# FNet mixing and a squared-ReLU layer on one core: the folds of a batch spread over three blocks, and P−Q+N taken on VectorE in other steps

## The chip, the cores and the metric

The kernel runs on one core of a Trainium2 chip. The metric is the device time of one execution, in microseconds (us). The profile is of one execution of the kernel before the change, taken by the hardware profiler. Its engines are PE (TensorE matmuls), PEld (TensorE weight loads), DVE (VectorE), ACT (ScalarE), POOL (GpSimd) and SP (SyncE, here the queue of output stores).

## The reference

```python
# x: 8 x 3008 x 256, w_in: 256 x 2048, w_out: 2048 x 256, all float32
X = np.fft.fft(x, axis=1)          # over the 3008 positions
X = np.fft.fft(X, axis=2)          # over the 256 features
t = X.real.reshape(8 * 3008, 256)
h = np.maximum(t @ w_in, 0.0)
out = h * h @ w_out                # 24064 x 256
```

## The kernel before, in words

**What is computed how.** The transform over the features is multiplied into `w_in` once, at the start (`gh`, 256 x 2048, as a cosine part, a sine part, and a third part `gh[:, 2]` that is minus twice the sine part but for one row). The transform over positions is done as matmuls with tables of cosines and sines, after the 3008 positions have been folded by symmetry (position n with position S−n, then the halves once more). Rows k and S−k of the result differ only in the sign of the sine product: with P the cosine product and Q the sine product, one row needs P+Q and the other P−Q, with a term N (the Nyquist feature) that keeps its sign. So only about half of the columns are computed, 12040 in all, and each column gives two output rows.

**Blocks and steps.** The columns are cut into 25 blocks ("windows" in the code, `wins`, index `w`): 240, 512, 512, 240, 512, 448 columns, then 18 blocks of 512, and a last one of 360. Each block has 8 steps `s` (`NST`), and a step makes 256 of the 2048 hidden features for all its columns: `phs[s]`, a PSUM tile `ph` of two banks, of which there are two. A step is written out in this order, and every engine works through its share of the program in order:

- A **plain step**: `pq` (two pairs of matmuls, lines 793 and 794, P+Q into `ph`); `settle` (VectorE squares what earlier steps left in the list `kept`, `power`, line 833, and what `held` kept back is done by `let_go`); `relu(s, 0)` on ScalarE (line 829); `others(s)`, see below; `turn` (two matmuls, line 816, which add the third part and so make P−Q+N); `relu(s, 1)` on ScalarE. That is six matmuls of the block's width. In step 7 the first half is squared at once, ahead of `others(7)`, and only the second half goes to `kept`.
- A **step in `diff[w]`** takes P−Q+N on VectorE: `cosines` (two matmuls, line 802, P alone); `twice` on VectorE (line 806: `t2` = n2 − 2P, from PSUM); `settle`; `others(s)`; `sines` (two matmuls, line 811, which wait for `twice`, since they add Q to the tile that it reads); `relu(s, 0)` on ScalarE; `relu(s, 1)` on VectorE (line 827: `t2` + (P+Q), cut at zero). That is four matmuls, and the second ScalarE operation is gone. The tile `n2` is made by GpSimd, two operations a step (line 739, in `nyq_rows`), from a row that a matmul with `sel` spreads over the partitions (line 730) and ScalarE copies (line 731), in step 6 of the block before (`hi`) for the first step of `diff`, and in step 7 for the others. There are three buffers for `n2`.
- **`others(s)`**: the fold jobs `at[s]`; then 16 matmuls (line 678, `ffn2_steps`) of the second layer for 128 rows of the block before, whose sum ScalarE copies out every second step (line 693) and SP stores; then `post[s]`; then a share of the position transform of the next block (`z_steps`, line 565, copies on ScalarE, and `minus` on VectorE, line 594), spread over the steps from `lo` up to, not including, `hi`.

**The folds.** The columns of a batch i (order in the code, 0 to 7) come in two units, (i, 0) and (i, 1). For i from 2 on, unit (i, 0) begins in block b0 + 2 where b0 is 5, 8, 10, 13, 16 and 19. The jobs of `fold_steps(i)` are: `d_even` (lines 417 to 419), `n_cos` (427), `d_odd` (422; it ends by issuing the load of the next batch's x on GpSimd's queue, lines 127 to 150), `n_sin` (430), `odds` (433), `nyq` (438 to 440: two tiny matmuls and a copy), `even` (445, and a write to scratch memory in DRAM on GpSimd's queue, 447), `back` (four reads of it on the same queue, 455 and 457, which wait for the write), and the four `late` jobs (471 twice, 482 twice, and with the last the small copies of lines 488 to 490), which need what `back` read. Before the change all but the late ones lie in block b0: `d_even`, `n_cos`, `d_odd`, `n_sin` in steps 0 to 3, `odds` in 5, `even` and then `nyq` in 6, `back` in 7. The late jobs lie in steps 2, 4, 6 and 7 of the second block ahead of the unit (i, 1): blocks 6, 9, 12, 15, 18, 21 (`late_at`).

**Which steps are in `diff`:** (4, 6) in block 4, (5,) in the fold blocks b0, and (2, 4, 6) in all others from block 6 on: 50 steps.

Of the kernel before, what the change touches and what calls it, by code (L numbers as in the profile page):

```python
# [29 lines left out]
def kernel(  # L30
# [15 lines left out]
    B, S, D = x.shape  # L46
    _, F = moe_w_in.shape
# [7 lines left out]
    NFC = F // P  # L55
# [24 lines left out]
    NW = len(wins)  # L80

    def win_of(col):
        return max(w for w in range(NW) if wins[w][0] <= col) if col < TOT else NW
# [5 lines left out]
    col_of = {}  # L89
# [218 lines left out]
    at = const.tile([P, 2, P + 1], F32, name="at")  # L308
# [228 lines left out]
    held = {"on": False, "jobs": []}  # L537

    def let_go():
        jobs, held["jobs"] = held["jobs"], []  # L540
        for j in jobs:
            j()
# [167 lines left out]
    folds = {0: f0s}  # L710

    def fold_jobs(i):
        f = folds[i] = fold_steps(i)
        return [f["d_even"], f["n_cos"], f["d_odd"], f["n_sin"], f["odds"], f["nyq"], f["even"], f["back"]]

    fold_at, late_at = {}, {}
    for i in range(2, B):
        fold_at[win_of(col_of[i, 0]) - 2] = i
        late_at[win_of(col_of[i, 1]) - 2] = i
    NST = NFC // 2  # L720
    diff = {w: (4, 6) if w == 4 else (5,) if w in fold_at else (2, 4, 6) for w in range(4, NW)}
    n2s = {}
    BIG = 3.0e38
    zns = {}

    def spread_nyq(wt):
# [15 lines left out]
    for w in range(NW):  # L742
        g0, wn = wins[w]
        h2 = h2p.tile([P, NFC, 2 * WN], F16, name="h2", tag="h2")
        zcw, zsw = zwin(w)

        lo, hi = 0, NST - 2
        at = [[] for _ in range(NST)]
        post = [[] for _ in range(NST)]
        if w == 0:  # L750
            at[0] = [lambda: gh_step(2, True), lambda: gh_turn(2), f0s["v_even"]]
            at[2] = [lambda: gh_step(3, False), lambda: gh_turn(3)]
            rm = z0(0, 2) + z0(1, 2)
            at[4] = rm[0::2]
            at[5] = rm[1::2]
        elif w == 1:
            fj = fold_jobs(1)
            at = [[], fj[0:1], fj[1:2], fj[2:3], fj[3:5], [], [], []]
            post[5] = fj[5:6]
            lo, hi = 6, NST  # L760
        elif w == 2:
            te = table_steps(1)
            at = [[folds[1]["even"]], [lambda: te["freq"](), lambda: te["args"](0)], [lambda: f0s["v_part"](0)], [lambda: f0s["v_part"](1), f0s["even"], f0s["back"]],
                  [lambda: te["turns"](0)], [lambda: te["mods"](0)], [lambda: te["absm"](0), lambda: te["sins"](0)], [lambda: te["coss"](0)]]
        elif w == 3:
            at[0] = [lambda: te["weigh"]()]
            for st in range(4):
                at[1 + st // 2] = at[1 + st // 2] + f0s["late"][st : st + 1]
            at[3] = [folds[1]["back"]]
            lo, hi = 4, NST  # L770
        elif w in fold_at:
            fj = fold_jobs(fold_at[w])
            at = [[f] for f in fj[0:4]] + [[], fj[4:5], fj[6:7], fj[7:8]]
            post[6] = fj[5:6]
        elif w == win_of(col_of[1, 1]) - 1:
            for st in range(4):
                at[1 + st] = folds[1]["late"][st : st + 1]
            lo, hi = 5, NST
        if w in late_at:
            for st in range(4):  # L780
                at[(2, 4, 6, 7)[st]] += folds[late_at[w]]["late"][st : st + 1]
        zj, zl = [], []
        for u in need[w + 1]:
            zu = z_steps(u)
            zj += [(zu, 1, 0), (zu, 0, 0), (zu, 1, 1), (zu, 0, 1)]
        f2 = ffn2_steps(*old) if old else []
        phs = {}

        def pq(s):
            ph = phs[s] = ps_h.tile([P, 2, 512], F32, name="ph", tag="psh")  # L790
            for a in range(2):
                f0 = (2 * s + a) * P
                nc.tensor.matmul(ph[:, a, 0:wn], gh[:, 0, f0 : f0 + P], zcw[:, 0:wn], start=True, stop=False)  # L793
                nc.tensor.matmul(ph[:, a, 0:wn], gh[:, 1, f0 : f0 + P], zsw[:, 0:wn], start=False, stop=True)  # L794

        t2s = {}

        def cosines(s):
            ph = phs[s] = ps_h.tile([P, 2, 512], F32, name="ph", tag="psh")
            for a in range(2):  # L800
                f0 = (2 * s + a) * P
                nc.tensor.matmul(ph[:, a, 0:wn], gh[:, 0, f0 : f0 + P], zcw[:, 0:wn], start=True, stop=True)  # L802

        def twice(s):
            t2 = t2s[s] = tmp.tile([P, 3 * NE], F32, name="t2", tag="tt")[:, 0 : 2 * WN].rearrange("p (a n) -> p a n", a=2)
            nc.vector.scalar_tensor_tensor(out=t2[:, :, 0:wn], in0=phs[s][:, :, 0:wn], scalar=-2.0, in1=n2s[w, s][:, :, 0:wn], op0=ALU.mult, op1=ALU.add)  # L806

        def sines(s):
            for a in range(2):
                f0 = (2 * s + a) * P  # L810
                nc.tensor.matmul(phs[s][:, a, 0:wn], gh[:, 1, f0 : f0 + P], zsw[:, 0:wn], start=False, stop=True, skip_group_check=True)  # L811

        def turn(s):
            for a in range(2):
                f0 = (2 * s + a) * P
                nc.tensor.matmul(phs[s][:, a, 0:wn], gh[:, 2, f0 : f0 + P], zsw[:, 0:wn], start=False, stop=True, skip_group_check=True)  # L816

        def relu(s, sg):
            h = h2[:, 2 * s : 2 * s + 2, sg * wn : (sg + 1) * wn]
            if sg:  # L820
                h = rev_dim(h, 2)
            if w == 1 and not sg:

                for a in range(2):
                    nc.scalar.activation(h[:, a], phs[s][:, a, 0:wn], AF.Relu, bias=0.0, scale=-1.0)  # L825
            elif sg and s in t2s:
                nc.vector._custom_dve(TENSOR_ADD_SAT, out=h, in0=t2s[s][:, :, 0:wn], in1=phs[s][:, :, 0:wn], s0=BIG, s1=0.0)  # L827
            else:
                nc.scalar.activation(h, phs[s][:, :, 0:wn], AF.Relu, bias=0.0, scale=-1.0)  # L829

        def power(s, a, b):
            h = h2[:, 2 * s : 2 * s + 2, a * wn : b * wn]
            nc.vector.tensor_tensor(h, h, h, op=ALU.mult)  # L833

        def others(s):
            for j in at[s]:
                j()
            for j in spread(f2, s, NST):
                j()
            for j in post[s]:  # L840
                j()
            if s == lo:
                zl[:] = [j for zu, part, h in zj for j in zu(part, h)]
            if s >= lo:
                for j in spread(zl, s - lo, hi - lo) if s < hi else []:
                    j()

        def nyq(s):
            if w + 1 in diff and hi < NST - 1:
                if s == hi:  # L850
                    spread_nyq(w + 1)
                    nyq_rows(w + 1, diff[w + 1][0:1])
                elif s == hi + 1:
                    nyq_rows(w + 1, diff[w + 1][1:])
            if s == 0 and w in diff and w not in zns:
                spread_nyq(w)
                nyq_rows(w, diff[w])

        kept = []

        def settle():
            for k in kept:
                power(*k)
            kept.clear()
            let_go()

        ng = 2 if w == 0 else 1
        for s0 in range(0, NST, ng):
            ss = range(s0, s0 + ng)
            held["on"] = s0 + ng in diff.get(w, ())  # L870
            if s0 in diff.get(w, ()):
                cosines(s0)
                twice(s0)
                settle()
                others(s0)
                sines(s0)
                relu(s0, 0)
                relu(s0, 1)
                kept.append((s0, 0, 2))
                nyq(s0)  # L880
                continue
            for s in ss:
                pq(s)
            settle()
            for s in ss:
                relu(s, 0)
                if s == NST - 1:
                    power(s, 0, 1)
            for s in ss:
                others(s)  # L890
            nyq(s0)
            for s in ss:
                turn(s)
            for s in ss:
                relu(s, 1)
                kept.append((s, int(s == NST - 1), 2))
        held["on"] = False
        settle()
        if w == 0:
            gh_nyq()  # L900
        old = (w, h2)
# [32 lines left out]
```

## Time and profile before

| | |
|---|---|
| median of three runs | 625.15 us (625.14 to 625.29) |
| the profiled execution: time, span | 625.18 us, 623.4 us |
| PE busy | 599.6 us (96%), 4487 matmuls |
| DVE busy | 464.3 us (74%) |
| ACT busy | 423.3 us (68%) |
| POOL busy | 257.1 us (41%) |
| clock granted to TensorE | 0.998 |

Times in the profile count from the start of the span. The profiled execution takes 1.78 us more than its span, and 0.03 us more than the median. Matmuls are pipelined: the duration of one (379 ns for 512 columns) is longer than the distance to the next, so work on PE is costed by the distance between starts. "Idle before" is what the engine waited ahead of a group, and the arrow names what ended that wait.

### The profile page before, as it was taken

The page shows a single profiled execution, that of the slowest core. Times are in us where ns is not written, and L with a number is a line of the kernel's source. Part 1 is how long each engine was busy: PE and PEld are TensorE (multiplying, and loading weights), DVE is VectorE, ACT ScalarE, POOL GpSimd, SP SyncE. Part 2 cuts the span into 40 slices and gives each one's busy share as a digit, 9 for nine tenths or more (in the row PEclk, how much of TensorE's full clock was granted, in tenths as well). Part 3 has the DMA queues.
Part 4 walks back from the last instruction along what each step waited for, and adds up shares of the span by engine and source line. Part 5 has one row for each costly group of instructions (what it writes and reads, how often), then busy time and mean ns, then how long its engine had stood idle before and what let it go on. Part 6 is the DMA issues. An engine that isn't in the chain of part 4 may idle for free.

```text
span 623.4 us, 11238 instructions
## 1 busy us (share of the span) xinstructions
PE 599.6 (96%) x4487; PEld 431.3 (69%) x4487; DVE 464.3 (74%) x567; ACT 423.3 (68%) x589; POOL 257.1 (41%) x202
## 2 busy tenths in 40 slices
PE   4789998899999999999999999999999999999997
PEld 2456686577677777777777777776777777777786
DVE  7686753886978869768788679876797787876761
ACT  6677766767767666776677675776667767666652
POOL 8302322356452292255422942347610446426310
PEclk9999999999999999999999999999999999999999
DMA  8746331136111731541116411173111221211112
GB/s 151 106 99 142 103 95 35 33 68 163 49 46 34 150 99 50 109 124 49 52 46 121 119 47 43 44 143 102 50 29 62 68 79 34 51 44 37 53 54 68
DMA packets 36539, 47.51 MB, mean 76 GB/s; under 512 B 4231, under 2 KB 30343, under 8 KB 36487
## 3 DMA queue, kind: packets, MB, share of 16 engines
q0 software_dynamic: 9344, 22.14, 17.8%
q1 hardware_dynamic: 26915, 24.44, 13.1%
q8 instruction: 35, 0.57, 0.4%
q10 hardware_dynamic: 228, 0.21, 0.1%
q14 instruction: 17, 0.14, 0.1%
HBM read 33.63 MB, written 27.84 MB: 99 GB/s over the span
## 4 chain that ended last, share of the span: by engine, by line
PE 86%; ACT 5%; DVE 3%; POOL 3%; DMA 1%; issue 1%; POOLq 0%; DVEq 0%
PE po L678 49%; PE ph L816 9%; PE ph L793 9%; PE ph L794 9%; PE pz L565 3%; PE ph L811 3%; PE ph L802 3%; ACT h L829 3%; DMA scr<-ev 1%; ACT h L825 1%; DVE t L806 1%; PE pn L730 1%; POOL n L739 1%; DVE h L833 1%; PE pg L511 0%
## 5 line engine op out<-in xcount | busy, mean ns | idle before, releaser
L829 ACT ACTIVATE h<-ph 128x1024 f16<-128x1024 f32 (+3 forms) x342 | 317.3, 968 | 83.4 <-PE ph L816 39.7
L678 PE MATMUL po<-wout,h 128*128 128x256 f16 (+1 forms) x3024 | 361.6, 273 | 0.0
L678 PEld LDWEIGHTS <-h 128*128 128x128 f16 (+1 forms) x3024 | 296.5, 98 | 71.6
L833 DVE TENSOR_TENSOR h<-h 128x2048 f16<-128x2048 f16 (+7 forms) x225 | 235.4, 1057 | 80.8 <-ACT h L829 78.8
L739 POOL TENSOR_SCALAR n<-zn,g2n 128x512 f32<-128x512 f16 (+2 forms) x100 | 179.5, 1810 | 169.4 <-ACT zn L731 169.0
L793 PE MATMUL ph<-zc,gh 128*128 128x512 f16 (+3 forms) x300 | 108.0, 363 | 5.4 <-DVE zc L594 2.2
L794 PE MATMUL ph<-zs,gh 128*128 128x512 f16 (+3 forms) x300 | 108.0, 363 | 0.0
L693 ACT ACTIVATE osb<-po 128x512 f32<-128x512 f32 (+2 forms) x94 | 54.9, 587 | 64.3 <-PE po L678 50.8
L816 PE MATMUL ph<-zs,gh 128*128 128x512 f16 (+3 forms) x300 | 84.2, 363 | 3.4 <-ACT h L825 1.9
L806 DVE SCALAR_TENSOR_TENSOR t<-ph,n 128x1024 f32<-128x1024 f32 (+2 forms) x50 | 60.1, 1203 | 33.3 <-PE ph L802 30.2
L827 DVE CUSTOM_DVE_ANT_0 h<-t,ph 128x1024 f16<-128x1024 f32 x46 | 56.1, 1220 | 16.6 <-ACT h L829 15.3
L794 PEld LDWEIGHTS <-gh 128*128 128x128 f16 x300 | 29.3, 98 | 37.4 <-issue 6.7
L793 PEld LDWEIGHTS <-gh 128*128 128x128 f16 x300 | 29.2, 98 | 31.0 <-DVE h L827 0.2
L816 PEld LDWEIGHTS <-gh 128*128 128x128 f16 x300 | 27.5, 97 | 12.2 <-issue 6.0
L447 POOL DMA_DIRECT2D scr<-ev x8 | 4.8, 596 | 65.9 <-DVE od L440 49.2
L811 PE MATMUL ph<-zs,gh 128*128 128x512 f16 (+2 forms) x100 | 29.3, 374 | 1.6 <-DVE t L806 1.6
L802 PE MATMUL ph<-zc,gh 128*128 128x512 f16 (+2 forms) x100 | 29.3, 375 | 0.0
L127 POOL DMA_DIRECT2D xo<-in_x_dram x8 | 6.3, 782 | 52.9 <-DVE fo L422 42.4
L570 ACT ACTIVATE es<-pz 128x376 f32<-128x376 f32 (+1 forms) x32 | 15.3, 483 | 13.8 <-PE pz L565 13.7
L132 POOL DMA_INDIRECT xo<-in_x_dram,idx_r x15 | 21.1, 1407 | 4.5 <-issue 4.3
L457 POOL DMA_INDIRECT rb<-scr,idx_r x16 | 19.8, 1237 | 4.9 <-issue 4.9
L802 PEld LDWEIGHTS <-gh 128*128 128x128 f16 x100 | 9.8, 98 | 11.4
(134 smaller groups left out, 338.5 us busy)
## 6 DMA issues: line engine op xcount, KB each, us to landing
out_dram<-osb SPq DMA_DIRECT2D x77, 128.0 KB
xo<-in_x_dram POOLq DMA_DIRECT2D x7, 768.0 KB, 6.7
scr<-ev POOLq DMA_DIRECT2D x8, 390.0 KB, 3.7
rb<-scr POOLq DMA_DIRECT2D x16, 130.0 KB
out_dram<-osb SPq DMA_DIRECT2D x12, 94.0 KB
w<-in_moe_w_in_dram POOLq DMA_DIRECT2D x2, 512.0 KB
wout<-in_moe_w_out_dram POOLq DMA_DIRECT2D x1, 1024.0 KB
out_dram<-osb SPq DMA_DIRECT2D x8, 75.0 KB
```

The source lines that it names most:

```text
L678: nc.tensor.matmul(po[0:m, j * D : (j + 1) * D], h2[:, fc, q : q + m], wout16[:, fc, :], start=(fc == 0), stop=(fc == NFC - 1))
L693: nc.scalar.activation(osb[0:mm].rearrange("p s d -> p (s d)")[:, lo:hi], po[0:mm, lo:hi], AF.Copy, bias=0.0, scale=HS * HS)
L739: nc.gpsimd.tensor_scalar(out=n2[:, a, 0:wn1], in0=zns[wt][:, 0:wn1], scalar1=g2n[:, fc : fc + 1], scalar2=None, op0=ALU.mult)
L793: nc.tensor.matmul(ph[:, a, 0:wn], gh[:, 0, f0 : f0 + P], zcw[:, 0:wn], start=True, stop=False)
L794: nc.tensor.matmul(ph[:, a, 0:wn], gh[:, 1, f0 : f0 + P], zsw[:, 0:wn], start=False, stop=True)
L802: nc.tensor.matmul(ph[:, a, 0:wn], gh[:, 0, f0 : f0 + P], zcw[:, 0:wn], start=True, stop=True)
L806: nc.vector.scalar_tensor_tensor(out=t2[:, :, 0:wn], in0=phs[s][:, :, 0:wn], scalar=-2.0, in1=n2s[w, s][:, :, 0:wn], op0=ALU.mult, op1=ALU ...
L811: nc.tensor.matmul(phs[s][:, a, 0:wn], gh[:, 1, f0 : f0 + P], zsw[:, 0:wn], start=False, stop=True, skip_group_check=True)
L816: nc.tensor.matmul(phs[s][:, a, 0:wn], gh[:, 2, f0 : f0 + P], zsw[:, 0:wn], start=False, stop=True, skip_group_check=True)
L827: nc.vector._custom_dve(TENSOR_ADD_SAT, out=h, in0=t2s[s][:, :, 0:wn], in1=phs[s][:, :, 0:wn], s0=BIG, s1=0.0)
L829: nc.scalar.activation(h, phs[s][:, :, 0:wn], AF.Relu, bias=0.0, scale=-1.0)
L833: nc.vector.tensor_tensor(h, h, h, op=ALU.mult)
```

## The change

The jobs of the folds are placed by two tables made before the loop, `at_of` and `post_of`, and so are the steps in `diff`. For batch 2 all stays as it was. For batches 3 to 7:

- `d_even` and `n_cos` go to steps 0 and 1 of the block ahead of b0: blocks 7, 9, 12, 15, 18.
- `d_odd` (with the load of x), `n_sin`, `odds`, `even`, `back` lie in steps 0, 1, 2, 3 and 6 of b0, and `nyq` behind step 3's matmuls of the second layer.
- The late jobs lie in block b0 + 1, in steps 2, 4, 6, 7: blocks 9, 11, 14, 17, 20.
- `diff` is (4, 6) in the blocks b0 and in block 9; (2, 4, 6) elsewhere; and (0, 2, 4, 6) in the last four blocks, 21 to 24. Together that is 58 steps.
- Where the next block has step 0 in `diff`, `hi` is 5 instead of 6 (so in blocks 20 to 23 the position transform is spread over five steps, and the rows of `n2` begin in step 5), and the `settle` at the end of the block is left out: the second half of step 7 is squared behind the next block's first `twice`. For that `kept` outlives a block.

```diff
-    fold_at, late_at = {}, {}
+    NST = NFC // 2
+    at_of = {w: [[] for _ in range(NST)] for w in range(NW)}
+    post_of = {w: [[] for _ in range(NST)] for w in range(NW)}
+    diff = {w: (2, 4, 6) for w in range(4, NW)}
+    diff[4] = (4, 6)
...
     for i in range(2, B):
-        fold_at[win_of(col_of[i, 0]) - 2] = i
-        late_at[win_of(col_of[i, 1]) - 2] = i
-    NST = NFC // 2
-    diff = {w: (4, 6) if w == 4 else (5,) if w in fold_at else (2, 4, 6) for w in range(4, NW)}
+        b0 = win_of(col_of[i, 0]) - 2
+        early = i > 2
+        late = b0 + 1 if early else win_of(col_of[i, 1]) - 2
+        a0 = b0 - 1 if early else b0
+        at_of[a0][0].append(lambda i=i: make(i))
+        put(at_of, a0, 0, (i, "d_even"))
+        put(at_of, a0, 1, (i, "n_cos"))
+        if early:
+            for s, name in ((0, "d_odd"), (1, "n_sin"), (2, "odds"), (3, "even"), (6, "back")):
+                put(at_of, b0, s, (i, name))
+            put(post_of, b0, 3, (i, "nyq"))
+            diff[b0] = (4, 6)
+        else:
+            for s, name in ((2, "d_odd"), (3, "n_sin"), (5, "odds"), (6, "even"), (7, "back")):
+                put(at_of, b0, s, (i, name))
+            put(post_of, b0, 6, (i, "nyq"))
+            diff[b0] = (5,)
+        for st in range(4):
+            at_of[late][(2, 4, 6, 7)[st]].append(lambda i=i, st=st: folds[i]["late"][st]())
+        if early and any(late == win_of(col_of[j, 0]) - 3 for j in range(3, B)):
+            diff[late] = (4, 6)
+    for w in range(NW - 4, NW):
+        diff[w] = (0, 2, 4, 6)
...
-        lo, hi = 0, NST - 2
-        at = [[] for _ in range(NST)]
-        post = [[] for _ in range(NST)]
+        lo, hi = 0, NST - 3 if 0 in diff.get(w + 1, ()) else NST - 2
+        at, post = at_of[w], post_of[w]
...
-            held["on"] = s0 + ng in diff.get(w, ())
+            held["on"] = s0 + ng in diff.get(w, ()) or (s0 + ng == NST and 0 in diff.get(w + 1, ()))
...
-                kept.append((s0, 0, 2))
+                keep(s0, 0, 2)
...
-        held["on"] = False
-        settle()
+        if w + 1 not in diff or 0 not in diff[w + 1]:
+            settle()
```

More of the change, by code (lines that the diff above doesn't have):

```diff
@@ L714, in fold_jobs, with put, make, settle @@
         return [f["d_even"], f["n_cos"], f["d_odd"], f["n_sin"], f["odds"], f["nyq"], f["even"], f["back"]]
-    fold_at, late_at = {}, {}
-    for i in range(2, B):
-        fold_at[win_of(col_of[i, 0]) - 2] = i
-        late_at[win_of(col_of[i, 1]) - 2] = i
-    NST = NFC // 2
-    diff = {w: (4, 6) if w == 4 else (5,) if w in fold_at else (2, 4, 6) for w in range(4, NW)}
+    NST = NFC // 2
[3 more added lines that the diff above has]
+    diff[4] = (4, 6)
+    def put(d, w, s, j):
+        d[w][s].append(lambda: folds[j[0]][j[1]]())
+    def make(i):
+        folds[i] = fold_steps(i)
+    for i in range(2, B):
+        b0 = win_of(col_of[i, 0]) - 2
[21 more added lines that the diff above has]
+        diff[w] = (0, 2, 4, 6)
     n2s = {}
     BIG = 3.0e38
+    kept = []
+    def settle():
+        for k in kept:
+            k()
+        kept.clear()
+        let_go()
     zns = {}
@@ L770 @@
             lo, hi = 4, NST
[L771 to L774, printed above, removed]
         elif w == win_of(col_of[1, 1]) - 1:
             for st in range(4):
-                at[1 + st] = folds[1]["late"][st : st + 1]
+                at[1 + st] += folds[1]["late"][st : st + 1]
             lo, hi = 5, NST
-        if w in late_at:
-            for st in range(4):
-                at[(2, 4, 6, 7)[st]] += folds[late_at[w]]["late"][st : st + 1]
         zj, zl = [], []
@@ L829, in relu, with keep, power @@
                 nc.scalar.activation(h, phs[s][:, :, 0:wn], AF.Relu, bias=0.0, scale=-1.0)
-        def power(s, a, b):
+        def keep(*k):
+            kept.append(lambda p=power: p(*k))
+        def power(s, a, b, h2=h2, wn=wn):
             h = h2[:, 2 * s : 2 * s + 2, a * wn : b * wn]
@@ L857, in nyq @@
                 nyq_rows(w, diff[w])
[L859 to L865, printed above, removed]
         ng = 2 if w == 0 else 1
@@ L895 @@
                 relu(s, 1)
-                kept.append((s, int(s == NST - 1), 2))
-        held["on"] = False
-        settle()
+                keep(s, int(s == NST - 1), 2)
+        if w + 1 not in diff or 0 not in diff[w + 1]:
+            settle()
         if w == 0:
```

## The prediction

> **What bounds the kernel now.** First the page: busy shares and the 40 slices.
>
> ```profile
> PE 599.6 (96%) x4487; PEld 431.3 (69%) x4487; DVE 464.3 (74%) x567; ACT 423.3 (68%) x589; POOL 257.1 (41%) x202
> ...
> PE   4789998899999999999999999999999999999997
> ```
>
> PE is full from the fifth slice on; only its own work and its waits count. Next the view of waits, for what PE waits for in a step of `diff`:
>
> ```profile
> DVE t L806 <- PE ph L802: 30.2, 36, 1.6
> ...
> PE ph L811 <- DVE t L806: 1.6, 4, 0.5
> ```
>
> VectorE waits for the cosines (36 times), PE hardly ever for `twice`: 1.6 us in 50 steps. Then PE's timeline in block 21, for the price of a step:
>
> ```profile
> 520.11 0.38 PE L793 MATMUL ph<-zc,gh 128*128 128x512 f16 x1
> ...
> 523.15 0.59 PE L802 MATMUL ph<-zc,gh 128*128 128x512 f16 x2
> ...
> 525.76 0.38 PE L793 MATMUL ph<-zc,gh 128*128 128x512 f16 x1
> ```
>
> A plain step lasts 523.15 − 520.11 = 3.04 us, one in `diff` 525.76 − 523.15 = 2.61: it saves 0.43. In block 24 (360 columns) the starts lie 2.66 and 2.36 apart: 0.30. Then the timeline of all engines in block 23, for the loop behind such a step:
>
> ```profile
> 576.48 0.59 PE L802 MATMUL ph<-zc,gh 128*128 128x512 f16 x2
> ...
> 577.18 1.22 DVE L806 SCALAR_TENSOR_TENSOR t<-ph,n 128x1024 f32<-128x1024 f32 x1
> ...
> 578.66 0.59 PE L811 MATMUL ph<-zs,gh 128*128 128x512 f16 x2
> ...
> 579.29 1.94 ACT L829 ACTIVATE h<-ph 128x1024 f16<-128x1024 f32 x2 [1.48 <-PE ph L811]
> ...
> 580.35 1.22 DVE L827 CUSTOM_DVE_ANT_0 h<-t,ph 128x1024 f16<-128x1024 f32 x1 [0.81 <-ACT h L829]
> ...
> 581.60 1.23 DVE L833 TENSOR_TENSOR h<-h 128x2048 f16<-128x2048 f16 x1
> 582.13 0.59 PE L802 MATMUL ph<-zc,gh 128*128 128x512 f16 x2
> ...
> 582.83 1.23 DVE L806 SCALAR_TENSOR_TENSOR t<-ph,n 128x1024 f32<-128x1024 f32 x1
> ```
>
> `twice` starts 0.70 behind the cosines and ends at 1.93; the sines start at 2.18. In the four places where PE did wait, the sines came 0.05 behind `twice`. So `twice` may come 0.20 late for nothing; from there on its lateness is PE's. (Position matmuls in the step add their length to that slack.) The loop back is tight: sines, the first ReLU on ScalarE, line 827, the square (ends 582.83), and the next `twice` at that moment, two steps later. Here a `diff` step every second step just fits.
>
> **The PE work removed.** By blocks, 512 columns wide: 8, 10, 13, 16 and 19 go from one `diff` step to two (+5), block 9 from three to two (−1), 21 to 23 from three to four (+3): seven net, 7 × 0.43 = 3.01 us. Block 24 gains one: 0.30. Sum **−3.31 us**, all on the path. ScalarE loses eight ReLUs of 1.02 us, which shortens nothing; VectorE gains eight pairs of 1.22 + 1.22, and GpSimd eight pairs of `n2` rows (1.83 us each on average), priced below by what waits for them.
>
> **A stall that goes.** The chain of waits around 430 us, in block 17:
>
> ```profile
> 428.25 4.10 POOL n L739 x2
> ...
> 432.37 1.24 DVE t L806
> ...
> 433.65 0.59 PE ph L811 x2
> ```
>
> In block 16 x was loaded late (GpSimd 403.65 to 413.75), the write of scratch behind it landed only at 424.1, `back` waited for that in front of the `n2` rows, and `twice` in step 4 started 1.17 late. Block 17 lasted 25.82 us where its like (11, 14, 20) lasts 25.16: 0.66 lost. After the change `d_odd` is in step 0: it ends about 3.8 us into block 16, and the load begins 403.65 − 396.0 = 7.6 us earlier. The write then lands at about 416.5, or 24.4 us into a block of 24.9. `back` (four issues, 3.8 us) now stands ahead of all `n2` rows of block 17, so the first pair (4.10 us) is ready 7.75 us into it; its `twice`, in step 2, is due at 2 × 3.36 + 0.70 = 7.42 and, with 0.32 us of position matmuls in the step, may be 0.52 late. No stall, by 0.2 us: **−0.66**. The later rows have 2 us and more. Blocks 8, 10, 13 have shorter loads and 4 us or more to spare; 19 loads nothing.
>
> **The folds.** At the start of a block behind one with late jobs, VectorE in block 10 (which begins at 244.64) did what blocks 12, 15 and 18 will do:
>
> ```profile
> 243.90 1.82 DVE L833 TENSOR_TENSOR h<-h 128x2048 f16<-128x2048 f16 x2
> 245.64 0.83 DVE L482 TENSOR_TENSOR xy<-xy 128x520 f16<-128x520 f16 x1
> ...
> 246.68 0.68 DVE L833 TENSOR_TENSOR h<-h 128x1024 f16<-128x1024 f16 x1
> ...
> 250.44 0.96 DVE L427 TENSOR_TENSOR ab<-fe 128x1560 f16<-128x1560 f16 x1
> ```
>
> `n_cos` is through at 251.33, 6.69 us into the block (an instruction starts about 0.08 before the last one's end). `twice` of step 2 there is due at 2 × 3.04 + 0.70 = 6.78, and harmless until 6.98. Cost 0, cover 0.29 us. In 7 the first steps are longer (6.42 for the two), and block 9 has no `diff` step before 4. In the b0 blocks step 3 holds a square, `even` (0.97) and the copy of `nyq`, through some 0.4 us into step 4, where `twice` is due at 0.70: 0. The tile of `nyq` makes the next sum of the second layer wait for ScalarE's copy of step 3; that copy ends about 0.2 us into step 4 and the sum begins at 0.43: 0. The late jobs with a position transform beside them are block 9's case of before, where PE never idled; the extra `minus` in block 20's step 4 (five steps instead of six) makes step 6's `twice` some 0.1 late: 0.
>
> **The new step 0.** `twice` of step 0 stands in VectorE's queue behind the square of step 7's first half, which stands behind the loop of step 6. With the spreading matmul now in step 5, line 827 of step 6 starts 1.26 us into step 7; the square follows at 2.51, the half square at 3.65, and VectorE is free 0.60 later: 4.25, or 1.21 into the next block instead of 0.70. It is 0.51 late, and PE waits 0.51 − 0.20 = 0.31 in block 23. Block 22's step 0 has 0.25 of position matmuls: 0.06. Block 24: `twice` takes 0.91, so it ends at 2.12, and the sines come at 2.17 instead of 0.30 + 1.75 = 2.05: 0.12. Block 21 is worse: step 7 of block 20 now holds the last late jobs, between the half square and `twice`. From the half square to the end of those copies took 246.68 − 245.04 = 1.64 in block 9, so `twice` starts at 0.61 + 1.64 = 2.25 and ends at 3.48, the sines come at 3.53 instead of 2.18: 1.35. Together **+1.84 us**. Behind `twice` are queued the second half square (needed four steps later) and line 827: nobody is late from that.
>
> **Sum**: −3.31 − 0.66 + 1.84 = −2.13. The profiled execution took 625.18 (span 623.4), the median is 625.15, so no correction: 625.18 − 2.13 = 623.05, about **623.1 us**.
>
> [...] VectorE's squares of 2048 take 1.22 us beside no `n2` row and at most 1.49 beside one; the rows take 1.6 alone and up to 2.64. So GpSimd yields, and VectorE loses 0.27 at worst, 0.07 beyond the slack: I add nothing. [...]
>
> **The rivals.**
> 1. *Only the gain.* If the boundary waits don't come (line 827 earlier, the small copies hidden), it is −3.31 − 0.66: 621.2 us. Against it stands the in-order queue; for it that PE so rarely waited. Chance 0.13.
> 2. *The folds cost too.* The covers of 0.29 (blocks 12, 15, 18) and 0.2 (block 17) are thin. A square lengthened by 0.27 and a late ScalarE copy make up to 0.4 in each of three blocks: 1.2 us more, 624.3. Chance 0.22.
> 3. *Slower: GpSimd's queue in block 16.* If the write of scratch lands later than 24.6 us into the block, each us more delays block 17's first `n2` pair, its `twice` and PE by a us, since `back` now stands ahead of that pair. It turns the sign 2.3 us behind the estimated 24.4. If only half of the load's 7.6 us of earliness reaches the write (other transfers in its way), it lands 3.8 late, PE loses 3.6, and the time is 623.05 + 3.6 = 626.7. For it: this queue did stall PE here. Against: nothing else on GpSimd's queue has moved ahead of the load. Chance 0.06.
> 4. *VectorE is held whole rows long.* If a row already running held a square for 1.6 us, a tight loop would lose 1.6 − 0.2 = 1.4; half of the 16 new rows hitting gives 11 us, 634. The 48 squares that ran beside rows speak against it. Chance 0.03.
>
> That the change doesn't do what it says can be left out: the written order of PE has 16 matmuls fewer.
>
> **How the numbers follow.** The forecast has 0.56, its own range 622.4 to 623.8 (the waits of step 0 between half and one and a half times their price). A measurement here can tell about 0.2%, 1.25 us: faster means under 623.9. That is the forecast, rival 1, and 0.05 of rival 2's mild end: 0.74. Within: the rest of rival 2 and half of rival 3: 0.20. Slower: the other half and rival 4: 0.06. The range reaches from rival 1 to rival 2, 621.1 to 624.6, and leaves out 0.09 and the ends of the two.
>
> **What would show it.** 58 steps with line 806's counterpart; PE idle behind `twice` at the starts of blocks 21 (1.3 us), 23 (0.3) and 24 (0.1); none in 17; block 8 at 23.7 instead of 24.17. It is wrong if PE waits in blocks 11 to 19, or if the wait at 21 is absent.

## The result, and the profile after

The changed kernel takes 634.95 us (median of four runs, 632.16 to 636.97) against 625.14 us before: a ratio of 1.0153, 95% interval [1.0115, 1.0192]. It is 1.5% slower; the forecast was 0.3% faster. The profiled execution is the longest of the four: it took 636.97 us with a span of 635.2 us, 11.8 us more than the span of before, while the medians differ by 9.8. The account below is of that one execution. The page's busy shares:

```profile
PE 601.8 (95%) x4471; PEld 431.3 (68%) x4471; DVE 486.4 (77%) x583; ACT 416.3 (66%) x581; POOL 309.5 (49%) x218
...
PE   4789998899999999999999899997999999999996
```

The 16 matmuls are gone, and yet PE is busy 2.2 us longer, and two slices in the middle are under 9 that were full before. POOL is busy 52 us more for 16 more rows of `n2`. The view of waits has lines that were not there before:

```profile
POOL rb L455 <- DMA scr<-ev: 44.5, 6, 11.6
...
DVE t L836 <- POOL n L777: 12.1, 2, 6.8
...
PE ph L841 <- DVE t L836: 10.7, 9, 4.5
```

GpSimd stood 44.5 us in front of `back`, waiting for the write of scratch (7.5 before); VectorE's `twice` (line 836 now) waited twice for `n2` rows, 12.1 us in all; and PE waited 10.7 us for `twice` (1.6 before). Where that is, the chain of waits around 350 us (block 14) says:

```profile
338.69 8.43 DMA scr<-ev
347.12 0.28 issue
347.40 1.10 POOL rb L455 x2
...
350.27 0.98 POOL rb L457
351.26 0.04 issue
351.30 3.13 POOL n L777 x2
354.43 0.02 issue
354.45 1.24 DVE t L836
355.69 0.04 issue
355.73 1.01 PE ph L841 x2
```

Scratch lands at 347.1, `back` is issued, the first pair of rows follows, then `twice`, then the sines. PE's timeline of the same place:

```profile
349.97 0.59 PE L832 MATMUL ph<-zc,gh 128*128 128x512 f16 x2
...
355.73 1.01 PE L841 MATMUL ph<-zs,gh 128*128 128x512 f16 x2 [3.09 <-DVE t L836]
356.54 0.63 PE L823 MATMUL ph<-zc,gh 128*128 128x512 f16 x1
356.96 0.63 PE L824 MATMUL ph<-zs,gh 128*128 128x512 f16 x1
...
358.24 2.26 PE L678 MATMUL po<-wout,h 128*128 128x256 f16 x16
```

PE idles for 3.09 us, and then its matmuls of 512 columns start 0.43 us apart instead of 0.22. Step 2 lasts 6.56 us instead of 2.93 and step 3 4.56 instead of 3.36. In block 17 these two steps last 7.97 and 5.51, behind a longer wait:

```profile
435.70 1.01 PE L841 MATMUL ph<-zs,gh 128*128 128x512 f16 x2 [4.50 <-DVE t L836]
```

Lengths of the blocks, from the starts of their first matmuls in PE's timelines, account for all of it:

| blocks | before, us | after, us | difference |
|---|---|---|---|
| 14 | 25.16 | 30.00 | +4.84 |
| 17 | 25.82 | 32.36 | +6.54 |
| 12, 15, 18, each | 23.25 | 23.66 | +0.41 |
| 10, 13, 16, 19, each | 25.34 | 24.91 | −0.43 |
| 8; 9 | 24.17; 25.16 | 23.74; 25.60 | −0.43; +0.44 |
| 21; 22; 23 | 23.25; 24.42; 23.19 | 24.30; 24.05; 23.06 | +1.05; −0.37; −0.13 |
| 24 with the tail | 35.46 | 35.85 | +0.39 |

The sum is +11.8. The tail, from the start of the last step to the end of the span, lasted between 17.7 and 18.5 us in the profiles of all the kernels here, which have the same program there; what makes it vary stays open.

### The profile page after: what moved, and what is told of

Read it like the earlier page. It is cut to its first block, busy times and chain, and to the rows that moved or that the text cites. A ratio compares the mean times of both kernels' runs of the same rounds, so it can differ in the third digit from the quotient of the medians.

```text
span 635.2 us, 11247 instructions
## 1 busy us (share of the span) xinstructions
PE 601.8 (95%) x4471; PEld 431.3 (68%) x4471; DVE 486.4 (77%) x583; ACT 416.3 (66%) x581; POOL 309.5 (49%) x218
## 4 chain that ended last, share of the span: by engine, by line
PE 66%; POOL 11%; ACT 6%; issue 6%; DMA 6%; DVE 5%; POOLq 0%; DVEq 0%
PE po L678 37%; POOL n L777 8%; PE ph L846 6%; PE ph L823 6%; PE ph L824 6%; PE ph L841 3%; DMA scr<-ev 3%; ACT h L859 3%; PE pz L565 3%; PE ph L832 3%; DVE t L836 2%; DVE h L866 2%; DMA xo<-in_x_dram,idx_c 1%; ACT h L855 1%; DMA xo<-in_x_dram,idx_f 1%
## 5 line engine op out<-in xcount | busy, mean ns | idle before, releaser
L859 ACT ACTIVATE h<-ph 128x1024 f16<-128x1024 f32 (+3 forms) x334 | 310.6, 967 | 104.3 <-PE ph L841 61.6
L777 POOL TENSOR_SCALAR n<-zn,g2n 128x512 f32<-128x512 f16 (+2 forms) x116 | 232.6, 2021 | 160.8 <-ACT zn L769 149.1
L823 PE MATMUL ph<-zc,gh 128*128 128x512 f16 (+3 forms) x284 | 103.0, 366 | 5.4 <-DVE zc L594 2.2
L824 PE MATMUL ph<-zs,gh 128*128 128x512 f16 (+3 forms) x284 | 103.1, 367 | 0.0
L836 DVE SCALAR_TENSOR_TENSOR t<-ph,n 128x1024 f32<-128x1024 f32 (+2 forms) x58 | 69.5, 1198 | 31.1 <-PE ph L832 18.9
L857 DVE CUSTOM_DVE_ANT_0 h<-t,ph 128x1024 f16<-128x1024 f32 x53 | 64.7, 1220 | 25.3 <-ACT h L859 24.9
L846 PE MATMUL ph<-zs,gh 128*128 128x512 f16 (+3 forms) x284 | 79.5, 363 | 3.4 <-ACT h L855 1.9
L824 PEld LDWEIGHTS <-gh 128*128 128x128 f16 x284 | 27.9, 98 | 36.3 <-issue 7.8
L823 PEld LDWEIGHTS <-gh 128*128 128x128 f16 x284 | 27.9, 98 | 29.8 <-issue 1.1
L841 PE MATMUL ph<-zs,gh 128*128 128x512 f16 (+2 forms) x116 | 34.7, 381 | 10.9 <-DVE t L836 10.7
L455 POOL DMA_DIRECT2D rb<-scr x16 | 8.9, 559 | 54.0 <-DMA scr<-ev 44.5
L846 PEld LDWEIGHTS <-gh 128*128 128x128 f16 x284 | 26.0, 97 | 11.9 <-issue 6.0
L832 PE MATMUL ph<-zc,gh 128*128 128x512 f16 (+2 forms) x116 | 33.9, 374 | 0.0
L570 ACT ACTIVATE es<-pz 128x376 f32<-128x376 f32 (+1 forms) x32 | 15.3, 483 | 13.6 <-PE pz L565 11.6
L841 PEld LDWEIGHTS <-gh 128*128 128x128 f16 x116 | 10.9, 98 | 14.8 <-issue 12.7
L832 PEld LDWEIGHTS <-gh 128*128 128x128 f16 x116 | 11.3, 98 | 13.3
```

The lines of the kernel that those rows point to most:

```text
L777: nc.gpsimd.tensor_scalar(out=n2[:, a, 0:wn1], in0=zns[wt][:, 0:wn1], scalar1=g2n[:, fc : fc + 1], scalar2=None, op0=ALU.mult)
```

## The experiments

The theory that these traces suggest is about GpSimd's queue. The rows of the second `diff` step of a fold block now stand ahead of the load of x, so the load is late, scratch behind it lands late, `back` holds the queue, and the next block's first rows are late. Here is that queue at the start of block 13, first in the changed kernel (where the block begins at 318.35), then in the kernel before (318.40):

```profile
316.89 9.41 POOL L777 TENSOR_SCALAR n<-zn,g2n 128x512 f32<-128x512 f16 x4 [11.03 <-ACT zn L769]
326.25 0.79 POOL L127 DMA_DIRECT2D xo<-in_x_dram  x1
```

```profile
316.95 3.90 POOL L739 TENSOR_SCALAR n<-zn,g2n 128x512 f32<-128x512 f16 x2 [13.12 <-ACT zn L731]
329.64 0.79 POOL L127 DMA_DIRECT2D xo<-in_x_dram  x1 [8.79 <-DVE fo L422]
```

Before, two rows, and the load waited for VectorE's `d_odd`. After, four rows of 2.35 us each, and the load, free to go at about 322.2 when `d_odd` ended, waits for them until 326.25. In block 16 of the changed kernel, which begins at 396.91, it is the same; `d_odd` ends there at 400.7, and line 132 is the first issue of that load:

```profile
395.45 9.41 POOL L777 TENSOR_SCALAR n<-zn,g2n 128x512 f32<-128x512 f16 x4 [11.02 <-ACT zn L769]
405.02 2.02 POOL L132 DMA_INDIRECT xo<-in_x_dram,idx_f  x1 [0.16 <-issue]
```

**1. The second rows behind the load** (`later` holds blocks 8, 10, 13, 16, 19, with 0):

```diff
                 elif s == hi + 1:
-                    nyq_rows(w + 1, diff[w + 1][1:])
+                    if w + 1 not in later:
+                        nyq_rows(w + 1, diff[w + 1][1:])
+            if w in later and s == later[w]:
+                nyq_rows(w, diff[w][1:])
```

> Changed kernel, but in the fold blocks 8, 10, 13, 16, 19 the n2 rows of the second diff step are issued behind the load of x (in step 0 of that block) and not ahead of it (step 7 of the block before). Theory 'late load' (those rows, 9.4 us for the two pairs and done 7.9 us into the block, hold the load up on GpSimd's queue, so the write of scratch lands late, back waits, and the next block's first n2 pair is late): load at 3.9 us into blocks 13 and 16 instead of 8, the waits of 3.1 us in block 14 and 4.5 us in block 17 gone or under 0.6 us, the slow matmuls behind them gone too, time about 625 us (637 less 12). Rival 'order' (back standing ahead of the n2 rows is enough by itself): waits of over 2 us stay in 14 and 17, 632 us or more. Rival 'VectorE' (two diff steps beside folds overload it): no change, 635 us.

Measured: 625.68 us (624.87 to 627.0), ratio to the kernel before 1.0008 [0.9998, 1.0017]. GpSimd's timeline in blocks 13 and 14:

```profile
316.92 3.88 POOL L778 TENSOR_SCALAR n<-zn,g2n 128x512 f32<-128x512 f16 x2 [11.03 <-ACT zn L770]
322.46 0.79 POOL L127 DMA_DIRECT2D xo<-in_x_dram  x1 [1.66 <-DVE fo L422]
...
335.34 4.07 POOL L778 TENSOR_SCALAR n<-zn,g2n 128x512 f32<-128x512 f16 x2
339.37 0.63 POOL L447 DMA_DIRECT2D scr<-ev  x1
342.98 1.10 POOL L455 DMA_DIRECT2D rb<-scr  x2 [2.98 <-DMA scr<-ev]
```

The load begins at 322.46 and waits for `d_odd` again; `back` goes out at 342.98 instead of 347.40. Blocks 14 and 17 last 25.16 us each, with no idle time on PE. The order of two GpSimd jobs is worth 9 us (634.95 against 625.68, the medians). "Order" is refuted: `back` still stands ahead of the rows. So is "VectorE": the fold blocks still have two `diff` steps. A smaller wait took a place in block 13: the rows for its own step 6 now stand behind a load that holds the queue until 335.3, and PE waits 0.97 us there (the step lasts 3.96 instead of 2.83).

**2. `back` behind the rows**, the load late as before: `(7, "back")` instead of `(6, "back")` in the table of the early folds.

> Changed kernel with back in step 7 of the fold blocks instead of 6, so that the next block's first n2 pair stands ahead of it. 'Late load': the load is as late as before, so the first late fold (line 471, which needs what back read) waits on VectorE instead; twice of step 2 in block 17 is on time, a wait of 1 to 3 us appears in step 3 or 4 there and under 0.6 us in block 14; about 628 us. 'Order': both waits vanish wholly, about 625 us.

Measured: 626.94 us (one run, so the reading rests on its trace). Block 14 lasts 25.16, block 17 26.90. VectorE in block 17:

```profile
424.42 1.23 DVE L836 SCALAR_TENSOR_TENSOR t<-ph,n 128x1024 f32<-128x1024 f32 x1 [1.58 <-PE ph L832]
425.56 1.60 DVE L866 TENSOR_TENSOR h<-h 128x2048 f16<-128x2048 f16 x1
429.86 0.70 DVE L471 TENSOR_TENSOR xy<-rb 128x1040 f16<-128x1040 f16 x1 [2.70 <-DMA rb<-scr,idx_r]
430.48 1.21 DVE L857 CUSTOM_DVE_ANT_0 h<-t,ph 128x1024 f16<-128x1024 f32 x1
```

`twice` waits only for PE, so its rows are in time; now the late fold waits 2.70 us for what `back` read, and line 857 behind it frees its PSUM tile late (PE idles 1.58 us ahead of step 4, between 430.16 and 431.74, and its matmuls behind that wait start 0.22 apart). So the late landing has two ways to PE, and the order of `back` decides which one is taken first and at what price.

**3. One `diff` step in the fold blocks**: `diff[b0] = (4,)`.

> Changed kernel with only step 4 in diff in the fold blocks 8, 10, 13, 16, 19. PE gains five times 0.43 us = 2.15 us of work. 'Late load': no second pair of rows ahead of the load, load at 3.9 us into the block, no waits in 14 and 17: 637 - 12 + 2.2 = about 627 us. 'Order': the waits stay, about 637 to 639 us. 'VectorE' (the spread folds themselves): waits stay in part.

Measured: 627.28 us (one run). Blocks 14 and 17 last 25.16 us. The spread folds by themselves hold nothing up there; the second pair of rows did.

**4. PE kept busy**, with matmuls that nothing reads (`warm` is `{14: 14, 17: 20}`):

```diff
                 others(s0)
+                if s0 == 2 and w in warm:
+                    pd = ps_o.tile([P, 512], F32, name="pd", tag="po")
+                    for _ in range(warm[w]):
+                        nc.tensor.matmul(pd[:, 0:wn], gh[:, 0, 0:P], zcw[:, 0:wn], start=True, stop=True)
                 sines(s0)
```

> Changed kernel with matmuls added that nothing reads: 14 of 512 columns in step 2 of block 14 and 20 in step 2 of block 17, between the second layer's matmuls and the sines, which fill PE's idle time there (3.0 and 4.3 us of 3.1 and 4.5). Theory 'clock' (the idle time lowers TensorE's clock, and 1.6 and 2.7 us are lost in the matmuls behind it): step 3 of blocks 14 and 17 lasts 3.4 us as elsewhere, and the time falls by about 4 us against the changed kernel, to 631 to 633 us. Rival (step 3 is long since ScalarE or VectorE catch up): step 3 stays at 4.6 and 5.5 us, time unchanged or longer.

Measured: 632.15 us (631.97 to 633.68), ratio to the kernel before 1.0111 [1.0095, 1.0128], against 1.0153 [1.0115, 1.0192] for the changed kernel. The two intervals overlap, so the times alone do not tell the two apart; the traces do. PE's timeline of block 14:

```profile
353.92 3.19 PE L905 MATMUL pd<-zc,gh 128*128 128x512 f16 x14
357.19 0.59 PE L842 MATMUL ph<-zs,gh 128*128 128x512 f16 x2
357.62 0.38 PE L824 MATMUL ph<-zc,gh 128*128 128x512 f16 x1
```

The sines come as late as before (step 2 lasts 6.19 us), but the matmuls behind them start 0.22 apart, and step 3 lasts 3.36 in both blocks. The two blocks together lose 28.43 + 29.74 − 2 × 25.16 = 7.85 us instead of 12.04: in the profiled execution 4.2 us of the changed kernel's loss were TensorE's clock, which 34 matmuls without use kept up. The medians differ by 2.8 us. The other three runs of the changed kernel were shorter, and how long the clock stayed low in them is not known.

**5. The last four blocks alone**: `early = False`, so that folds and `diff` are those of before but for (0, 2, 4, 6) in blocks 21 to 24.

> Only the second part of the change: the folds and their diff steps as before the change, but (0, 2, 4, 6) in the last four blocks (54 diff steps). No load is left to be late behind block 16's, which stays as before. PE's work falls by 1.59 us (3 x 0.43 + 0.30). Waits by the queue of VectorE: 0.3 us at step 0 of block 21 (no late folds in block 20 now), 1.1 to 1.3 at block 22 (the late folds are in step 7 of block 21), 0.3 at 23, 0.1 at 24; block 17 keeps its 0.66. Sum +0.2 to +0.4: 625.1 to 625.6 us, no change that can be told. Rival (the last four blocks are part of the 10 us): over 627 us.

Measured: 625.49 us (625.42 to 626.95), ratio 1.0002 [0.9992, 1.0013]. Step 0 lasts 2.91 us in block 21, 4.09 in 22, 2.92 in 23: the waits of 0.30 and 1.2, moved with the late folds to where they were expected. This part by itself neither wins nor loses.

**6. The rows away from `d_even`, first try**: `later` also holds 12, 15 and 18, with 1.

> rows_after_load, and in blocks 12, 15, 18 the n2 rows of steps 4 and 6 issued in step 1 of the block itself, so that no rows run beside d_even. Theory 'held' (the 0.41 us lost in step 2 of each comes from n2 rows that hold VectorE: d_even's sum took 2.08 instead of 1.78 us there and the square behind it 1.63 instead of 1.22): those two back at 1.78 and 1.22, step 2 at 2.61 in all three, 1.2 us less than rows_after_load, and perhaps 0.2 lost in step 4 where the rows run now. Rival (n_cos ahead of twice is simply too much for the steps): step 2 stays at 3.02.

Measured: 625.69 us (one run), step 2 of blocks 12, 15, 18 at 3.02 as before. This is inconclusive: the edit moved the rows in the program's text, but nothing in GpSimd's queue lay between, so they ran at the same times.

**7. A mixed version**: experiment 6, with step 0 not in `diff` in block 21 (`range(NW - 3, NW)`) and `diff[13] = (4,)`.

> rows12, and step 0 not in diff in block 21 (1.47 - 0.43 = 1.04 us won, since the late folds no longer stand ahead of a twice), and only step 4 in diff in block 13 (its 1.13 us wait for the rows of step 6, queued behind the load, against 0.43 of PE's work: 0.70 won). 625.7 - 1.2 - 1.0 - 0.7 = about 622.8 us, 0.4% under the kernel before.

Measured: 623.86 us (623.7 to 624.21), ratio 0.9977 [0.9967, 0.9986]. Block 21 lasts 23.25, block 13 25.34 without a wait; the 1.2 us that experiment 6 should have won are missing, and so the time is 1.1 us over the expected 622.8.

**8. The rows away from `d_even`, with a wait**: experiment 7, and in step 1 of blocks 12, 15, 18 and ahead of the rows,

```diff
             if w in later and s == later[w]:
+                if s == 1:
+                    nc.scalar.activation(zns[w][:, 0:wn], zns[w][:, 0:wn], AF.Copy, bias=0.0, scale=1.0)
                 nyq_rows(w, diff[w][1:])
```

> best, where in blocks 12, 15, 18 ScalarE copies the spread row onto itself in step 1, so that the n2 rows of steps 4 and 6 can't start before some 6.6 us into the block (in rows12 the edit moved them in the text only: GpSimd waited for nothing and ran them when it did before). Theory 'held' (rows lengthen d_even's sum to 2.08 us and the square behind it to 1.63): 1.78 and 1.22 again, step 2 of the three blocks at 2.61 instead of 3.02, about 1.2 us less than best: 622.7 us. Rival (n_cos ahead of twice is too much even without rows): step 2 stays at 3.0, 623.9 us.

Measured: 622.71 us (622.67 to 623.21), ratio 0.9955 [0.9942, 0.9969]: the lowest median here, though experiment 9 can't be told from it. VectorE in block 12, first of the changed kernel, then of this one:

```profile
297.57 2.08 DVE L418 TENSOR_TENSOR fe<-xo 128x3072 f16<-128x3072 f16 x1
299.57 0.20 DVE L419 COPY fe<-xo 128x24 f16<-128x24 f16 x1
299.66 1.63 DVE L866 TENSOR_TENSOR h<-h 128x2048 f16<-128x2048 f16 x1
301.21 0.96 DVE L427 TENSOR_TENSOR ab<-fe 128x1560 f16<-128x1560 f16 x1
302.10 1.21 DVE L836 SCALAR_TENSOR_TENSOR t<-ph,n 128x1024 f32<-128x1024 f32 x1
```

```profile
297.75 1.78 DVE L418 TENSOR_TENSOR fe<-xo 128x3072 f16<-128x3072 f16 x1
299.45 0.20 DVE L419 COPY fe<-xo 128x24 f16<-128x24 f16 x1
299.54 1.22 DVE L869 TENSOR_TENSOR h<-h 128x2048 f16<-128x2048 f16 x1
300.67 0.97 DVE L427 TENSOR_TENSOR ab<-fe 128x1560 f16<-128x1560 f16 x1
301.66 1.23 DVE L839 SCALAR_TENSOR_TENSOR t<-ph,n 128x1024 f32<-128x1024 f32 x1
```

Without rows beside them the sum takes 1.78 and the square 1.22 again, and `twice` is on time: step 2 lasts 2.61 in blocks 12 and 18 (2.76 in 15). "Held" is shown: `n_cos` stands ahead of `twice` as before, and the wait is gone with the rows.

**9. `n_cos` behind `twice`**, in step 2 of blocks 12, 15, 18, with the rows where the change has them; the rest as in experiment 7.

> best, with n_cos of batches 5, 6, 7 in step 2 of blocks 12, 15, 18, behind twice, and the rows as in the changed kernel. 'Held': d_even's sum and the square stay at 2.08 and 1.63, but twice no longer has n_cos's 0.96 ahead of it and is on time: step 2 at 2.61, about 1.2 us less than best (up to 0.6 lost again in step 4, since line 857 and the square of step 2 come behind n_cos): 622.7 to 623.3 us.

Measured: 622.97 us (622.49 to 624.09), ratio 0.9963 [0.9949, 0.9976]. The sum and the square stay at 2.08 and 1.63, and step 2 lasts 2.61 in all three: the other way to the same 1.2 us, with nothing lost in step 4.

## Why the prediction was wrong

**The stall that goes: the step that failed.** The text had `d_odd` end 3.8 us into the block, and let the load begin there, "7.6 us earlier". `d_odd` did end there. But the change also gives the fold blocks a second `diff` step, whose rows are queued in step 7 of the block before, ahead of that load; the sum priced these rows only by who reads them, never by what stands behind them. The load began behind them, 7.9 us into block 13 and 8.1 into block 16. From there on the chain ran as written: in block 16 scratch landed 30.1 us into the block (24.4 was forecast: 4.3 us of the difference come from the start of the load, the rest from a load that itself took longer, for a reason that stays open), `back` waited, and the first rows of block 17 came 12.6 us into it (7.75 forecast). Experiment 1 is the test of the rest of the term: there the load of block 16 began 4.1 us into the block and scratch landed 24.1 us into it, as forecast, and the stall stayed away. "Blocks 8, 10, 13 have shorter loads and 4 us or more to spare" was wrong for 13 even without the rows: its load stops midway for a gather (7.0 us of waiting before, 8.2 after), and in the trace of before it took 11.6 us from its first issue to its last, against 10.1 in block 16. With the load freed, scratch still landed only 24.3 us into block 13. So the third rival came true in its wait, and at over three times its price: 7.2 us in block 17, where it allowed 3.6, and 4.8 in block 14, which it did not name. It looked for the lateness in other transfers; the larger part came from the rows. What it set against itself, that nothing else had moved ahead of the load on GpSimd's queue, was the error itself. The sign of being wrong that the prediction gave, PE waiting in blocks 11 to 19, is what the trace shows.

**The price of a wait.** The text counted PE's lateness at one for one. Of the 12.0 us that blocks 14 and 17 lose against 25.16 each, 7.6 are idle time and 4.4 the slow matmuls after it; experiment 4 bought back 4.2.

**The folds: cost 0 was wrong, by 0.41 in each of blocks 12, 15 and 18.** The cover of 0.29 was read off block 10, where no rows ran beside `d_even`. That rows lengthen a square by "0.27 at worst" was the worst of one schedule; beside five rows in a row (293.24 to 303.53 in block 12) it was 0.41, and `d_even`'s sum lost 0.30; together 0.71 against the cover of 0.29. Rival 2 had the size, and the lengthened square; the other half of the delay came from the sum and not from a ScalarE copy.

**What held.** The steps: 3.04 and 2.61, and −0.43 in blocks 8, 10, 13, 16, 19. The new step 0: 1.47, 0.06, 0.30 and 0.11 us in blocks 21 to 24 (1.35, 0.06, 0.31, 0.12 forecast). With the load freed, the old stall of 0.66 in block 17 went as forecast (25.16 in experiment 1). Experiment 1 misses the forecast of 623.05 by 2.6 us, and 2.5 of them are accounted for: 1.23 in blocks 12, 15 and 18, 1.13 in block 13, and 0.12 in block 21.

**Squares and rows beside each other.** Squares beside rows took up to 1.65 us in the changed kernel, 1.22 without; rows took up to 3.3 us, 1.55 alone. Both are longer than in the trace of before (at most 1.49 and 2.64), but no square was held for a whole row; the rows bear most of it. Rival 4 asked only whether whole rows are lost, and that was too coarse: 0.71 us, less than half of a row, was enough.

## What to carry to other kernels

When work is added to an in-order queue, ask not only who needs its result but what is queued behind it, above all DMA issues: two more operations on an engine half idle delayed a load by 4 us, and that cost 12 in the profiled execution. Read the cover of a step from a stretch in which everything runs beside it that will run there after the change. And TensorE's waits of 3.09 and 4.50 us cost more than their length here (4.4 us of slow matmuls behind the two), while one of 1.58 us did not; filling the long ones won 4.2 us back in the profiled execution, which is worth it if they can't be removed.

## What the runs showed of the hardware

TensorE's clock was at half behind the waits of 3.09 and 4.50 us, and at full behind one of 1.31 us in block 21 of the changed kernel (1.00 granted from 531.50 to 533.50) and one of 1.58 us in experiment 2 (1.00 granted behind that wait). The clock granted behind the first two of these, and, in the last row, after it came back (columns: stretch; busy us of PE, PEld, DVE, ACT, POOL; PEclk; DMA):

```profile
355.70:358.60 2.90, 2.87 (x8) 1.13 (x8) 2.71 (x3) 1.14 (x2) 2.90 (x2) 0.50 0.00 0
435.70:438.20 2.50, 2.50 (x6) 0.84 (x6) 2.31 (x3) 1.02 (x1) 2.50 (x2) 0.50 0.03 7
...
360.66:363.60 2.94, 2.94 (x25) 2.16 (x23) 1.88 (x3) 1.55 (x2) 1.50 (x1) 1.00 0.29 88
```

It stayed low for 3.3 us in block 14 and 5.2 in block 17 (from the distances of the starts). At 0.50 the matmuls of 512 columns start 0.43 us apart, at 1.00 0.22. No wait between 1.58 and 3.09 us was measured, so how much idle time it takes to halve the clock is not shown.

In the changed kernel, rows of 512 columns that GpSimd runs beside VectorE's TENSOR_TENSOR operations (the squares and sums) take 2.1 us on average and up to 3.3 instead of 1.55, which is how four of them came to 9.4 us.
